# Turning a job's rows between the steps of the job before: a mixture of experts on one Trainium2 core

## The chip, the core and the metric

The kernel runs on one core of a Trainium2 chip. A core has a matmul engine (TensorE, PE in the profile, with its weight loads as PEld), VectorE (DVE), ScalarE (ACT), GpSimd (POOL) and a queue engine (SyncE, SP), each with its own stream of instructions, done in order and tied to the others by semaphores. The metric is the time of one execution in microseconds of device time, as the median of some runs.

## The reference

First a spectral layer on x of 8 x 1856 x 256: a Fourier transform over the sequence, a complex 256x256 product with a bias, a soft threshold, and the transform back. Its 14848 rows then go through a mixture of 16 experts in 4 groups, one expert for each row:

```
g_idx = argmax(x @ w_group);        g_w = softmax weight of that group
e_idx = argmax(xg @ w_expert[g]);   e_w = softmax weight of that expert
h  = maximum(xg[mask_e] @ w1[g, e], 0.0)      # 256 -> 1024
ye = h @ w2[g, e]                             # 1024 -> 256
out[tok_idx] = (g_w * e_w)[:, None] * ye
```

All is float32. The kernel makes each fp32 product from high and low parts (names ending in h and l): high x high, high x low and low x high.

## The kernel before

Until about 470 us the spectral layer, the routing and the first rows of four experts run in an order written out as a string of letters. From there on one loop goes over 40 **jobs**; the order on every engine is that of the program text. A job is one expert (or a part of one) with a fixed number of rows. Jobs 0 to 39 have these rows, bars standing between experts: 256, 304 | 432 | 400 | 384, 384, 336 | 256, 256 | 384, 384, 320 | 384, 384, 288 | 256, 384, 336 | 256, 384, 288 | 256, 384, 288 | 256, 384, 256 | 256, 384, 256 | 256, 320, 256 | 256, 320, 256 | 416, 384 | 320, 384.

What job i does, in the order of the text:

- The **second layer** of job i-1 (`down`, L695 and L696) for its first two tiles of 128 rows; for some row counts it is done turned instead (`turned_g`, L717), whole, with `back_g` (L730, L736, L738) bringing the result back during the job after.
- The **first layer** of job i (`up_g`): 8 steps f = 0 to 7 of six matmuls each (L619). After each step ACT makes hh, the high half of the hidden rows (L624), and DVE hl, the low half (L627). The second layer needs all hh and hl.
- Between the steps: the **gathers** of job i+2 (`deal_g`; POOL reads rows from memory into xg, L560; SP then deals them to the tile xm in blocks of 32 rows by 8 to 16 DMAs, L572), and the **weight pieces**. `split_w` lists eight pieces for the next expert's weights, each a cast on ACT (L524) and a subtraction on DVE (L525). In jobs 3, 5, 7, 10, 13, 16, 19, 22, 25, 28, 31, 34 and 36 such a list starts. With 384 rows or more and no older pieces one is emitted behind every step, all eight within the job; with fewer rows one behind every second step, and the other four in the job after.
- Behind the loop: pieces left over, then `dma_next` (SP loads the next expert's weights into the buffers that the pieces were read from, L512, and its row list, L1107 and L1109), then `turn_rows` for job i+1: DVE transposes xm in blocks of 32x32 into xtf, in four instructions (L582), ACT casts xtf to xth (L588), DVE subtracts to xtl (L589). Both are the first layer's input in job i+1. From job 4 on all jobs get their rows so, which makes 36 groups of four transposes.
- Then the rest of the second layer of job i-1, its third tile, if there is one.

The first layer writes to five PSUM buffers in turn, xm and xg have two and three buffers, xtf has one, the raw weights two.

Of the kernel before, what the change touches and what calls it, by code (L numbers as in the profile page):

```python
# [136 lines left out]
def spectral_moe(ctx: ExitStack, tc: tile.TileContext, x, wri, bri, wgate, w1, w1q, w2, cst, out):  # L137
# [179 lines left out]
    moved, heads, turns, parked = [], [], [], []  # L317
# [124 lines left out]
    def drain(gen):  # L442
        for _ in gen:
            pass
# [90 lines left out]
    def fetch(mp, ids, bufs, rows=NPAD + 1, late=False):  # L535
        n = ids.n
        out_ = []
        for c0 in range(0, n, 2):
            w = min(2, n - c0)
            xg = mp.tile([128, 2, D], F32, name="xg", bufs=bufs)  # L540
            for c in range(w):
                m = ids.rows(c0 + c)
                ins = nc.gpsimd.indirect_dma_start(
                    out=xg[0:m, c, :], out_offset=None, in_=ys_d[0:rows, :],
                    in_offset=bass.IndirectOffsetOnAxis(ap=ids.gi[0:m, c0 + c:c0 + c + 1], axis=0))
                if late:
                    behind(ins, "stores of the early jobs go first")
            out_.append((xg, w, ids.rows(c0 + w - 1)))
        return out_
# [23 lines left out]
            yield  # L573
        res.append(xm.rearrange("p c b d -> p (c b) d"))

    def turn_rows(xm, ids):
        n = ids.rows()
        xt = xq.tile([128, 2, 8, 64], F32, name="xtf", bufs=1)
        for a_ in range(2):
            k = (n - 32 * a_ + 63) // 64  # L580
            for to in range(2):
                nc.vector.transpose(out=xt[64 * to:64 * to + 64, :, 0:k, 32 * a_:32 * a_ + 32].rearrange("f b c t -> f c b t"),  # L582
                                    in_=xm[64 * a_:64 * a_ + 64, 0:k, 64 * to:64 * to + 64].rearrange("t c (b f) -> t c b f", b=2))
        xth = xq.tile([128, 2, n], F32R, name="xth")
        xtl = xq.tile([128, 2, n], F32R, name="xtl")
        xt = xt.rearrange("p b c t -> p b (c t)")
        for ts in [slice(i, min(n, i + 256)) for i in range(0, n, 256)]:
            nc.scalar.copy(out=xth[:, :, ts], in_=xt[:, :, ts])  # L588
            nc.vector.tensor_tensor(out=xtl[:, :, ts], in0=xt[:, :, ts], in1=xth[:, :, ts].bitcast(F32), op=ALU.subtract)  # L589
        return xth, xtl  # L590

    def prep(mp, xgs, n, bufs=None):
        xth = mp.tile([128, 2, n], F32R, name="xth", bufs=bufs)
# [16 lines left out]
    def up_g(pp, xt2, n, wt, hs):  # L610
        xth, xtl = xt2
        w1h, w1l = wt[0], wt[1]
        for f in range(8):
            o = pp.tile([128, 512], F32, name="ph")
            fs = slice(f * 128, (f + 1) * 128)
            k = 0
            for ch in range(2):
                for a_, b_ in ((w1h, xth), (w1h, xtl), (w1l, xth)):
                    nc.tensor.matmul(o[:, :n], lhsT=a_[:, ch, fs], rhs=b_[:, ch, 0:n], start=k == 0, stop=k == 5)  # L619
                    k += 1  # L620
            hh, hl = hs
            cuts = [slice(i, min(n, i + 256)) for i in range(0, n, 256)]
            for cs in cuts:
                ins = nc.scalar.activation(out=hh[:, f, cs], in_=o[:, cs], func=AF.Relu)  # L624
            step_end[:] = [ins.ins.name]
            for cs in cuts:
                nc.vector.scalar_tensor_tensor(out=hl[:, f, cs], in0=o[:, cs], scalar=0.0, in1=hh[:, f, cs].bitcast(F32),  # L627
                                               op0=ALU.max, op1=ALU.subtract)
            yield
# [29 lines left out]
    def h_tiles():  # L659
        return hq.tile([128, 8, WIDE], F32R, name="hh"), hq.tile([128, 8, WIDE], F32R, name="hl")  # L660
# [44 lines left out]
    def down(*args):  # L705
        drain(down_g(*args))
# [37 lines left out]
    jobs = [(0, 0), (0, 1), (1, 0), (1, 1), (0, 2), (1, 2), (2, NF), (3, NF)]  # L744
# [671 lines left out]
    def of(k):  # L1416
        return [("r", (k, i)) for i in range(len(CUTS[k]))]

    def fixed(e):
        return [("l", (e, i)) for i in range(len(FCUTS[e]))]  # L1420

    jobs = fixed(3) + fixed(1) + fixed(2) + of(0) + fixed(0)
# [4 lines left out]
    raws, jids, jw, rids, ready = {}, {}, {}, {}, {}  # L1427
# [23 lines left out]
    prev, behind_, todo, ahead = None, iter(()), [], {}  # L1451
    DEALT = jobs.index(("r", (0, 0)))
    x2 = prep(xq, first[0], jids[0].rows())
# [5 lines left out]
    for i, (kind, q) in enumerate(jobs):  # L1459
        ids = jids[i]  # L1460
        if kind == "r":
            wt = wts["r", q[0]] = jw[i] if i in jw else wts["r", q[0]]
        else:
            wt = wts[q[0]] = jw[i] if i in jw else wts[q[0]]
        nxt = fetch(xp2, jids[i + 1], 3, late=i == 0) if i + 1 < DEALT else None
        rest, back = iter(()), behind_
        behind_ = iter(())
        if prev is not None:
            pids = prev[1]
            if turned(i - 1):  # L1470
                yt = xq.tile([128, 2, WIDE], F32, name="yt", bufs=1)
                rest = turned_g(psy, "py", prev[0], pids, prev[2], yt)
                drain(rest)
                behind_ = back_g(psy, "py", yt, pids, "out")
            else:
                n2 = min(2, pids.n)
                down(psy, "py", prev[0], pids, prev[2], "out", range(n2))
                rest = down_g(psy, "py", prev[0], pids, prev[2], "out", range(n2, pids.n))
        ready.pop(i, lambda: None)()
        gathers = iter(())  # L1480
        if DEALT <= i + 2 < len(jobs):
            if jobs[i + 2][0] == "r":
                k, part = jobs[i + 2][1]
                jids[i + 2] = rids[k][part]
            ahead[i + 2] = []
            gathers = deal_g(jids[i + 2], ahead[i + 2])
        every = 1 if todo or ids.rows() < 384 else 0
        if i in split_at:
            jw[split_at[i]], todo = split_w(raws.pop(split_at[i]))
        hs = h_tiles()  # L1490
        for f, _ in enumerate(up_g(psh, x2, ids.rows(), wt, hs)):
            if f % 2:
                next(back, None)
            else:
                next(gathers, None)
            if f % 2 or not every:
                emit(todo, 1)
            for _ in range(1 if i else 3):
                next(table, None)
        if i not in split_at or not every:  # L1500
            emit(todo, len(todo))
        if i == 0 or i in split_at:
            dma_next(i)
        if nxt is None and i + 1 < len(jobs):
            x2 = turn_rows(ahead.pop(i + 1).pop(), jids[i + 1])
        drain(gathers)
        drain(rest)
        prev = (hs, ids, wt)
        if nxt is not None:
            x2 = prep(xq, nxt, jids[i + 1].rows())  # L1510
# [11 lines left out]
    with tc.For_i(KF, nfx, 1) as iv:  # L1522
        rw, ids = flex_load(bass.ds(iv, 1))
# [7 lines left out]
        wt, ids = half_load(bass.ds(iv, 1))  # L1531
# [45 lines left out]
```

## Time and profile before

| | us |
|---|---|
| median of three runs | 1068.2 |
| the three runs | 1068.2, 1059.08, 1074.6 |
| the profiled execution | 1074.4 |
| its span, first to last instruction | 1072.6 |
| busy in the span: PE | 1024.9 (96%) |
| DVE | 742.3 (69%) |
| ACT | 484.4 (45%) |
| POOL | 434.0 (40%) |

The span is what the trace covers; the remaining 1.8 us of the profiled execution lie around it. Matmuls are pipelined and their ends are modelled, so the start times of two matmuls tell more than the busy time. In a timeline a row is: start, duration, engine, line, operation, output and input tiles with partitions and elements, number of instructions merged, and in brackets the idle time of the engine ahead of it with what ended it.

### The profile page before, as it was taken

What the parts mean: (1) busy time and instruction counts of PE and PEld (TensorE: products, weight loads), DVE (VectorE), ACT (ScalarE), POOL (GpSimd) and SP (SyncE); (2) the same over time, 40 slices, a digit from 0 to 9 for tenths busy, and PEclk for the clock granted to TensorE, in tenths of its full rate; (3) what the DMA queues carried; (4) which work ended last, traced back from release to release, by engine and by line L of the source; (5) the groups of instructions that cost most, each with busy time, mean ns of one, the idle gap of its engine ahead of it and who ended that gap; (6) DMA issues with size and microseconds to landing.
All of it is one profiled execution on the core that took longest, in us unless ns stands there. A gap on an engine that the chain in (4) does not pass through costs nothing.

```text
span 1072.6 us, 25269 instructions
## 1 busy us (share of the span) xinstructions
PE 1024.9 (96%) x9496; PEld 888.0 (83%) x9496; DVE 742.3 (69%) x1754; ACT 484.4 (45%) x1273; POOL 434.0 (40%) x600
## 2 busy tenths in 40 slices
PE   8999999999999999999999999999999999999996
PEld 4886767776867888889988899979998898999995
DVE  6879999999998665436566665665665656767652
ACT  2664645545636243234344444444544535445532
POOL 0120164465463657633235324334342343443432
PEclk9999999999999999989999999999998999999998
DMA  9402512412314320312342442433424244244210
GB/s 383 146 2 91 187 42 106 152 63 81 121 60 180 122 105 28 126 53 67 126 139 79 142 140 72 137 88 126 146 68 135 62 146 140 70 143 139 79 52 29
DMA packets 63407, 117.25 MB, mean 109 GB/s; under 512 B 20588, under 2 KB 44473, under 8 KB 56754
## 3 DMA queue, kind: packets, MB, share of 16 engines
q1 hardware_dynamic: 46450, 67.81, 19.7%
q0 software_dynamic: 11936, 30.79, 9.0%
q10 hardware_dynamic: 4896, 17.01, 4.1%
q8 instruction: 76, 1.25, 0.5%
q14 instruction: 49, 0.40, 0.1%
HBM read 71.37 MB, written 32.46 MB: 97 GB/s over the span
## 4 chain that ended last, share of the span: by engine, by line
PE 61%; DVE 17%; issue 8%; POOL 4%; DMA 3%; SPq 3%; ACT 2%; another core or an unknown queue 0%; ACTq 0%; POOLq 0%; DVEq 0%
PE ph L619 20%; PE py L695 8%; PE pw L887 5%; PE py L717 5%; PE py L696 4%; SPq L572 3%; PE ph L1047 2%; PE pw L869 2%; PE bank L805 2%; PE bank L911 2%; PE bank L929 2%; DVE big L525 2%; DVE hl L627 2%; PE bank L435 2%; DVE big L439 2%
## 5 line engine op out<-in xcount | busy, mean ns | idle before, releaser
L619 PE MATMUL ph<-xth,big 128*128 128x256 f32 (+8 forms) x1280 | 291.7, 312 | 3.8 <-ACT xth L588 3.0
L627 DVE SCALAR_TENSOR_TENSOR hl<-ph,hh 128x256 fp32r<-128x256 f32 (+8 forms) x528 | 167.6, 355 | 132.6 <-ACT hh L624 78.4
L624 ACT ACTIVATE hh<-ph 128x256 fp32r<-128x256 f32 (+8 forms) x528 | 151.2, 339 | 182.1 <-PE ph L619 134.0
L695 PE MATMUL py<-big,hh 128*128 128x512 f32 (+2 forms) x608 | 222.5, 404 | 1.9 <-ACT hh L624 1.4
L619 PEld LDWEIGHTS ph<-xth,big 128*128 128x128 f32 x1280 | 216.6, 188 | 7.6 <-ACT xth L588 5.0
L619 PE MATMUL ph<-xtl,big 128*128 128x256 f32 (+8 forms) x640 | 199.1, 311 | 2.8 <-DVE xtl L589 2.4
L669 POOL DMA_INDIRECT out_dram<-yo,si_r x92 | 92.6, 1006 | 251.0 <-DVE yo L701 204.7
L696 PE MATMUL py<-big,hl 128*128 128x256 f32 (+2 forms) x608 | 175.5, 289 | 5.2 <-DVE hl L627 4.8
L695 PEld LDWEIGHTS py<-big,hh 128*128 128x128 f32 (+2 forms) x608 | 115.7, 190 | 30.3 <-ACT hh L624 2.3
L560 POOL DMA_INDIRECT xg<-ys_d,gi_r x92 | 93.7, 1018 | 89.7 <-ACT hh L624 60.5
L696 PEld LDWEIGHTS py<-big,hl 128*128 128x128 f32 (+2 forms) x608 | 116.0, 191 | 10.4 <-DVE hl L627 10.1
L619 PEld LDWEIGHTS ph<-xtl,big 128*128 128x128 f32 x640 | 120.4, 188 | 5.1 <-DVE xtl L589 4.3
L717 PE MATMUL py<-hh,big 128*128 128x320 f32 (+4 forms) x320 | 75.2, 319 | 1.4 <-DVE yo L701 1.2
L588 ACT CAST xth<-xtf 128x512 fp32r<-128x512 f32 (+5 forms) x59 | 28.4, 518 | 106.6 <-DVE xtf L582 106.6
L582 DVE STREAM_TRANSPOSE xtf<-xm 64x384 f32<-64x384 f32 (+3 forms) x144 | 72.9, 506 | 3.4 <-DMA xm<-xg 2.0
L525 DVE TENSOR_TENSOR big<-xt,big 128x512 fp32r<-128x512 f32 x104 | 71.0, 682 | 5.7 <-ACT big L524 4.4
L853 POOL TENSOR_TENSOR xdl<-xd,xdh 128x512 fp32r<-128x512 f32 (+1 forms) x23 | 28.0, 1217 | 107.4 <-ACT xdh L846 87.1
L887 PE MATMUL pw<-wh,xh 128*128 128x256 f32 x240 | 66.6, 300 | 2.8 <-DVE pw L877 2.8
L524 ACT CAST big<-xt 128x512 fp32r<-128x512 f32 x104 | 65.4, 629 | 0.0
L892 ACT ACTIVATE big<-pw,nlam 128x512 f32<-128x512 f32 x60 | 41.3, 689 | 46.4 <-PE pw L887 45.5
L887 PE MATMUL pw<-wl,xh 128*128 128x256 f32 x240 | 62.0, 280 | 0.0
L887 PEld LDWEIGHTS pw<-wh,xh 128*128 128x128 f32 x240 | 45.1, 188 | 16.9 <-DVE pw L877 7.5
(263 smaller groups left out, 2004.1 us busy)
## 6 DMA issues: line engine op xcount, KB each, us to landing
xt<-in_w_dram SPq DMA_DIRECT2D x21, 1024.0 KB
ys_d<-ysb ACTq DMA_DIRECT2D x32, 512.0 KB
xt<-in_w1q_dram SPq DMA_DIRECT2D x13, 1024.0 KB
xm<-xg SPq DMA_DIRECT2D x290, 32.0 KB
big<-in_x_dram SPq DMA_DIRECT2D x8, 1024.0 KB
xt<-in_x_dram SPq DMA_DIRECT2D x8, 1024.0 KB
xm<-xg SPq DMA_DIRECT2D x144, 16.0 KB
xg<-ys_d,gi_r POOLq DMA_INDIRECT x92
```

Of the source, the lines that this page charges most:

```text
L524: nc.scalar.copy(out=wt[:, 2 * i, cs], in_=raws[i][:, cs])
L525: nc.vector.tensor_tensor(out=wt[:, 2 * i + 1, cs], in0=raws[i][:, cs], in1=wt[:, 2 * i, cs].bitcast(F32), op=ALU.subtract)
L560: ins = nc.gpsimd.indirect_dma_start(out=xg[0:m, c, :], out_offset=None, in_=ys_d[0:NPAD + 1, :], in_offset=bass.IndirectOffsetOnAxis(ap=i ...
L582: nc.vector.transpose(out=xt[64 * to:64 * to + 64, :, 0:k, 32 * a_:32 * a_ + 32].rearrange("f b c t -> f c b t"), in_=xm[64 * a_:64 * a_ + ...
L619: nc.tensor.matmul(o[:, :n], lhsT=a_[:, ch, fs], rhs=b_[:, ch, 0:n], start=k == 0, stop=k == 5)
L624: ins = nc.scalar.activation(out=hh[:, f, cs], in_=o[:, cs], func=AF.Relu)
L627: nc.vector.scalar_tensor_tensor(out=hl[:, f, cs], in0=o[:, cs], scalar=0.0, in1=hh[:, f, cs].bitcast(F32), op0=ALU.max, op1=ALU.subtract)
L669: ins = nc.gpsimd.indirect_dma_start(out=out, out_offset=bass.IndirectOffsetOnAxis(ap=ids.si[0:ids.rows(t), t:t + 1], axis=0), in_=ysb, in ...
L695: nc.tensor.matmul(o, lhsT=hh[:, f, ts], rhs=w2b[:, :, f, :], start=f == 0, stop=f == 7, skip_group_check=True)
L696: nc.tensor.matmul(o[:, 0:D], lhsT=hl[:, f, ts], rhs=w2h[:, f, :], start=False, stop=f == 7, skip_group_check=True)
L717: nc.tensor.matmul(o, lhsT=w_[:, f, ds_], rhs=h_[:, f, 0:n], start=f == 0 and h_ is hh and w_ is w2h, stop=f == 7 and h_ is hh and w_ is n ...
L887: ins = nc.tensor.matmul(y, lhsT=a_[:, h, k % 2, j], rhs=t[:, j, h], start=False, stop=a_ is xl and h == 1, skip_group_check=True)
```

## The change

`turn_rows` becomes a generator, `turn_g`, that yields after each of its four transposes and appends its result to a list. In each job it is made ahead of the first layer's loop and advanced by one behind steps 4, 5, 6 and 7, ahead of what `back`, the gathers and the pieces emit in that step. What is left of it, the cast to xth and the subtraction to xtl, follows right behind the loop, ahead of pieces left over and of `dma_next`.

```
-    def turn_rows(xm, ids):
+    def turn_g(xm, ids, res):
...
                 nc.vector.transpose(out=xt[...], in_=xm[...])
+                yield
...
-        return xth, xtl
+        res.append((xth, xtl))
...
         hs = h_tiles()
+        turns, turning = [], iter(())
+        if i + 1 in ahead:
+            turning = turn_g(ahead.pop(i + 1).pop(), jids[i + 1], turns)
         for f, _ in enumerate(up_g(psh, x2, ids.rows(), wt, hs)):
+            if f >= 4:
+                next(turning, None)
             if f % 2:
                 next(back, None)
...
+        drain(turning)
         if i not in split_at or not every:
             emit(todo, len(todo))
         if i == 0 or i in split_at:
             dma_next(i)
-        if nxt is None and i + 1 < len(jobs):
-            x2 = turn_rows(ahead.pop(i + 1).pop(), jids[i + 1])
+        if turns:
+            x2 = turns.pop()
         drain(gathers)
         drain(rest)
```

## Rows read from the trace of the kernel before

**Rows 1.** The page's costliest groups: busy, mean ns of one, idle before, releaser.

```profile
L619 PE MATMUL ph<-xth,big 128*128 128x256 f32 (+8 forms) x1280 | 291.7, 312 | 3.8 <-ACT xth L588 3.0
...
L619 PE MATMUL ph<-xtl,big 128*128 128x256 f32 (+8 forms) x640 | 199.1, 311 | 2.8 <-DVE xtl L589 2.4
...
L696 PE MATMUL py<-big,hl 128*128 128x256 f32 (+2 forms) x608 | 175.5, 289 | 5.2 <-DVE hl L627 4.8
...
L582 DVE STREAM_TRANSPOSE xtf<-xm 64x384 f32<-64x384 f32 (+3 forms) x144 | 72.9, 506 | 3.4 <-DMA xm<-xg 2.0
```

**Rows 2.** Timeline of PE: second layer of job 9, first layer of job 10.

```profile
604.17 0.39 PE L695 MATMUL py<-big,hh 128*128 128x512 f32 x1
...
609.70 0.28 PE L696 MATMUL py<-big,hl 128*128 128x256 f32 x1
610.93 0.44 PE L619 MATMUL ph<-xth,big 128*128 128x384 f32 x1 [0.96 <-ACT xth L588]
611.69 0.45 PE L619 MATMUL ph<-xtl,big 128*128 128x384 f32 x1 [0.31 <-DVE xtl L589]
611.97 0.51 PE L619 MATMUL ph<-xth,big 128*128 128x384 f32 x2
```

**Rows 3.** Timeline of DVE, jobs 8 and 9, up to job 10's transposes.

```profile
590.23 0.42 DVE L627 SCALAR_TENSOR_TENSOR hl<-ph,hh 128x256 fp32r<-128x256 f32 x1 [0.48 <-ACT hh L624]
...
591.01 0.69 DVE L525 TENSOR_TENSOR big<-xt,big 128x512 fp32r<-128x512 f32 x1
...
601.77 0.62 DVE L627 SCALAR_TENSOR_TENSOR hl<-ph,hh 128x256 fp32r<-128x256 f32 x2 [0.44 <-issue]
...
607.54 2.33 DVE L582 STREAM_TRANSPOSE xtf<-xm 64x384 f32<-64x384 f32 x4 [1.96 <-DMA xm<-xg]
```

**Rows 4.** Timeline of DVE, last steps of job 16.

```profile
718.58 0.61 DVE L627 SCALAR_TENSOR_TENSOR hl<-ph,hh 128x256 fp32r<-128x256 f32 x2
...
719.71 0.61 DVE L627 SCALAR_TENSOR_TENSOR hl<-ph,hh 128x256 fp32r<-128x256 f32 x2
```

**Rows 5.** Timeline of PE, second layer of job 16.

```profile
720.18 0.39 PE L696 MATMUL py<-big,hl 128*128 128x256 f32 x1 [0.52 <-DVE hl L627]
```

**Rows 6.** Timelines of DVE and PE: last hl of job 19, its user.

```profile
764.50 0.61 DVE L627 SCALAR_TENSOR_TENSOR hl<-ph,hh 128x256 fp32r<-128x256 f32 x2
...
765.70 0.28 PE L696 MATMUL py<-big,hl 128*128 128x256 f32 x1
```

**Rows 7.** Chain that ended last: start, duration, what; job 10's last row DMAs.

```profile
605.27 0.59 SPq L572
...
606.54 1.76 DMA xm<-xg
```

**Rows 8.** Timeline of SP's queue around job 8.

```profile
591.73 0.33 SPq L512 DMA_DIRECT2D xt<-in_w_dram  x1
...
594.39 35.39 SPq L572 DMA_DIRECT2D xm<-xg  x44
```

**Rows 9.** Timeline of SP's queue, jobs 32 to 36.

```profile
949.86 0.33 SPq L512 DMA_DIRECT2D xt<-in_w_dram  x1
...
988.26 0.33 SPq L512 DMA_DIRECT2D xt<-in_w_dram  x1
...
1001.81 1.22 SPq L572 DMA_DIRECT2D xm<-xg  x2
```

**Rows 10.** Timeline of DVE, steps 4 and 7 of job 36.

```profile
999.64 0.65 DVE L627 SCALAR_TENSOR_TENSOR hl<-ph,hh 128x256 fp32r<-128x256 f32 x2
...
1006.42 0.66 DVE L627 SCALAR_TENSOR_TENSOR hl<-ph,hh 128x256 fp32r<-128x256 f32 x2 [3.20 <-remote]
```

**Rows 11.** Stages of job 16's end: us, busy by engine, granted clock, DMA share.

```profile
716.00:720.70 4.70, 2.90 (x10) 1.60 (x11) 4.70 (x13) 3.43 (x11) 0.46 (x2) 1.00 0.25 53
720.70:724.70 4.00, 4.00 (x16) 3.44 (x15) 3.22 (x8) 1.22 (x3) 0.00 (x0) 0.57 0.64 209
```

**Rows 12.** Timeline of ACT, job 16, step 3.

```profile
713.28 0.55 ACT L624 ACTIVATE hh<-ph 128x256 fp32r<-128x256 f32 x2 [1.85 <-PE ph L619]
```

## The prediction

> **What bounds the kernel now.** I read the page first: TensorE (PE) against the others, then the rows of its first matmuls in each job, since the change hands them their input. The first layer and the second layer form one stream of matmuls on PE, and in the job stage hardly anything else ends last. What PE still waits for is in [rows 1]: 3.0 us for the high half of a job's input (L588), 2.4 us for the low half (L589), and 4.8 us for the low halves of the hidden rows (L627). Then I read PE by start times, because a booked idle time is shorter than what is lost. At the start of job 10 [rows 2] the matmul after 609.70 was due at 609.82, the third one, at 611.97, was due 2 x 0.173 later, at 610.17: 1.80 us are lost where the rows book 0.96 + 0.31. The same kind of wait, with 0.5 to 1.8 us, stands in front of eight jobs (6, 9, 10, 14, 16, 20, 29 and 36). Then I read VectorE (DVE) in the job before such a start, and the queue of SyncE (SP) that brings the rows it turns.
>
> **A. What moving the transposes can give back.** The path to a job's input is now: last hl of the job before, four transposes, cast on ScalarE (ACT), subtraction on DVE. Afterwards only the fourth transpose stands behind the last hl, so the path is shorter by three; one takes 506 ns on the mean [rows 1], for a job of 384 rows 2.33/4 = 0.58 us [rows 3]. Three, 1.5 us, are about what the eight waits are long. They go, except where DVE itself is late. Price: the 5.4 us of [rows 1], times 1.80/1.27 for what the rows don't book: 7.7 us. Ends: 0 (all of them are late by B) and 7.7. I take 7.7.
>
> The second half of the change, the split ahead of pieces left over, I cost at nothing. Where eight pieces are due in a job, all eight are emitted within the loop; where four are, the other four go into the next job's loop; the list is empty whenever the call behind the loop is reached. The cast on ACT and the subtraction on DVE so keep their place among other instructions, but for the last piece, which now comes behind the fourth transpose. No instruction is added or removed, and the transposes issue no DMA.
>
> **B. What stands behind the three transposes on DVE.** DVE works in the order of the program. Transposes 1 to 3 now run ahead of the hl of steps 5, 6 and 7, and the next second layer needs these. In a job with eight weight pieces DVE makes one hl and one piece per 1.13 us (718.58 to 719.71, [rows 4]), while PE feeds a step of 384 rows in 6 x 0.173 = 1.04 us, and a step of the second layer in 0.35. So DVE is behind at the end of each such job. In job 16 PE waits for exactly these hl, 0.52 us of 1.13 [rows 5]. Each transpose put there moves the end of the last hl, and so PE, by its own length. Jobs 5, 16, 22, 25 and 28 show such a wait at their end: 5 x 3 x 0.506 = 7.6 us. In job 19 the last hl starts at 764.50 and takes 0.61, PE needs it at 765.70 [rows 6]: 0.59 us to spare against 1.52, costs 0.93. Read in the same way job 13 has 0.1 to spare and pays 1.4, job 10 has 1.4 and pays 0.1. In sum 10.0. In the smaller jobs 8, 15, 21, 34 and 35 the same count (pieces every second step) gives 0.15 to 1.35 each, about 3.4 together, less certain. Ends: 5 (only the five, and a third absorbed by waits that are there anyway) and 13.4. I take 12. Nothing in other jobs: DVE rests 0.44 us per step in a job without pieces [rows 3], and most such jobs have a third tile of the job before behind their loop.
>
> **C. Rows that are not there yet.** This is the added wait: a transpose now waits for its rows in the middle of the loop, and behind it on DVE are queued the hl of steps 5 to 7 (PE waits for them), the pieces (the weight buffer and so SP's next weight load wait for them) and the yo additions. In the trace one group waits: job 10's, at 607.54, idle 1.96 for xm [rows 3]. The hl of step 4 starts at 601.77 there, and so the first transpose would stand from 602.4 to 607.5, as the DMAs that it reads are issued up to 605.27 and the last one lands 1.76 after 606.54 [rows 7]. Then transposes and hl alternate, 0.58 and 0.55: the last hl ends at 607.54 + 3 x 0.58 + 3 x 0.55 = 610.9. PE, which begins the second layer of job 9 at 604.17 [rows 2], needs it 7 x 0.35 + 0.23 later, at 606.9: 4.0 us. And the rows come later still. SP's second weight load of job 7 starts at 591.73 [rows 8], right behind the last piece, which starts at 591.01 and takes 0.69 [rows 3]; the DMAs of job 10's rows are behind it on the same queue, from 594.39. With four transposes in front of that piece, 4 x 0.58, less the 0.48 us that DVE rests ahead of 590.23 [rows 3], it ends 1.8 us later: 4.0 to 5.8. The same pattern is at 949.86 (rows for job 34) and at 988.26 (rows for job 37, last issued behind 1001.81) [rows 9]. In job 36 the first transpose would be due at 1000.3 and get its rows at about 1003.0; its last hl, now at 1006.42 after a 3.20 us gap of ACT [rows 10], comes 1.4 later by the same count (transpose 0.58, piece 0.60, hl 0.57 in turn), with the shift 3.2. Job 33: 0.4 to 2.0. Together 5.8 to 11.0; I take 9, as the piece's delay is sure and its passing on to the rows likely.
>
> [...]
>
> **Sum.** -7.7 + 12 + 9 = +13.3 us. The profiled execution took 1074.4 us, its span being 1072.6 with 1.8 around it; its successor would take 1087.7. The three runs have their median at 1068.2, 0.6% lower, and 13.3 us are carried over as they are: 1081.5 us, +1.2%. Runs of the same kernel differ by 15 us here, so about 2% is what a measurement can tell from no change.
>
> **Rivals.** First, the other side: the waits of A go and B and C don't come. Its place is DVE's rest: if the transposes fit into DVE's gaps in steps 4 to 7, and the rows are there, PE loses nothing: 1068.2 - 7.7 = 1060.5. It decides at one point, whether the last hl of a job ends before PE's eighth pair of the second layer. For it: the gaps of 0.44 us per step in the jobs without pieces, and the one of 3.20 us in job 36. Against it: DVE is busy 4.70 of 4.70 us in the tail of job 16 [rows 11], with PE waiting. Chance 0.17.
>
> Second, slower by more: the new waits are worth more than their length because TensorE's clock falls. [...] Against it: jobs 16, 22 and 25 pay this already, so that it can come anew only at the others. [...] Chance 0.17.
>
> Third, the change does not do what it says: waits of ACT and SP that are tied to time and not to DVE absorb B and C as well as A: 1068. For it: ACT itself is late in the middle of job 16, by 1.85 us at 713.28 [rows 12], though PE had gone on by then. Chance 0.12.
>
> Forecast: chance 0.54.
>
> **How the numbers follow.** 1081. The range goes from the first rival's time to the second's, 1060 to 1095, which also takes in the ends of A to C (5 + 5.8 - 7.7 = +3 and 13.4 + 11 - 7.7 = +17). Slower by over 2% is above 1089.6: most of the second rival and the forecast's upper end, 0.2. Faster by over 2%, below 1046.8, would need more than all of A: 0.02. The rest, 0.78.
>
> **What would show it.** Right: the transposes stand between the hl of steps 4 to 7; PE's idle ahead of L619 for L588 and L589 falls from 5.4 us to below 2; its idle ahead of L696 and L717 for L627 rises by more than 5; a transpose in job 9 waits for xm for over 4 us, one in job 36 for over 2; job 10's rows are issued later than 594 to 606, measured from the start of job 8. Wrong: the rows of job 10 are there at step 4 of job 9; or DVE's last hl in jobs 16, 22, 25 and 28 ends no later against PE than before.

## The result, and the profile after

The changed kernel takes 1079.6 us (median of four runs, 1077.4 to 1083.8) against 1068.5 us for the kernel before (median of four, three of them those on record ahead): a ratio of 1.0117 [1.0084, 1.015] (the quotient of the medians is 1.0104), 11 us slower, where 1081 (+13.3 us) was forecast. The two profiled executions stand only 3.0 us apart (spans 1072.6 and 1075.6), because the one of before lies above its median and the one of after below. So parts are compared place by place, and the size of the whole is taken from the medians. Lines of the code behind the new function have moved by one: L588, L589, L619, L627 and L696 of before are L589, L590, L620, L628 and L697 of after.

The page of the kernel after, costliest groups, which answer to [rows 1]:

```profile
L620 PE MATMUL ph<-xth,big 128*128 128x256 f32 (+8 forms) x1280 | 290.9, 311 | 0.7 <-ACT xth L607 0.7
...
L620 PE MATMUL ph<-xtl,big 128*128 128x256 f32 (+8 forms) x640 | 198.3, 310 | 0.4 <-DVE xtl L608 0.4
...
L697 PE MATMUL py<-big,hl 128*128 128x256 f32 (+2 forms) x608 | 177.8, 292 | 15.3 <-DVE hl L628 12.9
...
L582 DVE STREAM_TRANSPOSE xtf<-xm 64x384 f32<-64x384 f32 (+3 forms) x144 | 72.8, 506 | 19.8 <-DMA xm<-xg 16.4
```

Read the last column. What PE still waits for ahead of the first layer belongs to an earlier stage (L607, L608); the 3.0 + 2.4 us for a dealt job's input are gone. In exchange PE waits 12.9 us instead of 4.8 for the low halves of the hidden rows, and DVE itself stands 16.4 us instead of 2.0 in front of transposes whose rows haven't come. Those 16.4 us are five places: jobs 9 (4.20), 24 (2.08), 27 (2.17), 33 (4.36) and 36 (3.54).

Timeline of DVE after, jobs 8 and 9, the stretch of [rows 3]:

```profile
588.41 0.69 DVE L525 TENSOR_TENSOR big<-xt,big 128x512 fp32r<-128x512 f32 x1
...
598.45 0.62 DVE L628 SCALAR_TENSOR_TENSOR hl<-ph,hh 128x256 fp32r<-128x256 f32 x2 [0.43 <-ACT hh L625]
603.27 0.57 DVE L582 STREAM_TRANSPOSE xtf<-xm 64x384 f32<-64x384 f32 x1 [4.20 <-DMA xm<-xg]
603.77 0.58 DVE L628 SCALAR_TENSOR_TENSOR hl<-ph,hh 128x256 fp32r<-128x256 f32 x2
604.36 0.57 DVE L582 STREAM_TRANSPOSE xtf<-xm 64x384 f32<-64x384 f32 x1
604.97 0.62 DVE L628 SCALAR_TENSOR_TENSOR hl<-ph,hh 128x256 fp32r<-128x256 f32 x2
605.62 0.57 DVE L582 STREAM_TRANSPOSE xtf<-xm 64x384 f32<-64x384 f32 x1
606.22 0.62 DVE L628 SCALAR_TENSOR_TENSOR hl<-ph,hh 128x256 fp32r<-128x256 f32 x2
```

Timeline of PE after, second layer of job 9:

```profile
602.57 0.40 PE L696 MATMUL py<-big,hh 128*128 128x512 f32 x1
604.21 0.40 PE L697 MATMUL py<-big,hl 128*128 128x256 f32 x1 [1.24 <-DVE hl L628]
604.44 0.40 PE L696 MATMUL py<-big,hh 128*128 128x512 f32 x1
605.45 0.39 PE L697 MATMUL py<-big,hl 128*128 128x256 f32 x1 [0.61 <-DVE hl L628]
605.67 0.53 PE L696 MATMUL py<-big,hh 128*128 128x512 f32 x1
606.70 0.58 PE L697 MATMUL py<-big,hl 128*128 128x256 f32 x1 [0.51 <-DVE hl L628]
607.08 0.63 PE L696 MATMUL py<-big,hh 128*128 128x512 f32 x1
```

One transpose waits, and three hl stand behind it on DVE; PE stops in front of each of them. The L696 at 607.08 would have been due at 603.62 (602.57 and three pairs of 0.35): 3.46 us lost, of which the rows book 2.36. Then each pair takes 0.64 instead of 0.35 for a while. The view by stretches of the kernel after shows why (us, busy time of PE, PEld, DVE, ACT, POOL, granted clock, DMA share, GB/s):

```profile
600.00:607.50 7.50, 5.14 (x23) 3.73 (x22) 4.04 (x10) 1.06 (x4) 0.93 (x1) 0.89 0.27 63
607.50:613.00 5.50, 5.50 (x20) 4.81 (x19) 1.47 (x4) 1.78 (x4) 1.04 (x1) 0.54 0.21 54
613.00:620.00 7.00, 7.00 (x42) 7.00 (x41) 6.16 (x17) 6.30 (x19) 4.54 (x5) 1.00 0.18 56
```

Behind the stretch in which PE was busy for 5.14 of 7.50 us the granted clock is 0.54 of full speed for 5.5 us, and 1.00 in the stretch after that: by estimate 0.46 x 5.5 = 2.5 us more. A wait of 3.5 us has cost 6.

The queue of SP after, around job 8, which starts at 577.13 here and at 581.89 before:

```profile
589.13 0.33 SPq L512 DMA_DIRECT2D xt<-in_w_dram  x1
...
591.79 38.55 SPq L572 DMA_DIRECT2D xm<-xg  x44
```

Counted from the start of job 8 the rows begin at 14.7 us, before at 594.39 - 581.89 = 12.5 [rows 8]: 2.2 us later. The piece that releases the weight load (DVE at 588.41, ending 589.10) now has four transposes ahead of it, and the load starts right behind its end. But job 9 itself starts as much later (15.3 us after job 8, before 13.1), because job 8's second layer takes 9.64 us instead of 7.48: it waits for hl behind transposes too. Against job 9's own start the rows begin 0.6 us ahead in both kernels. So in this execution the 4.20 us come from the early place alone; where the changed kernel was run again (experiment 11) the rows begin 0.96 us behind job 9's start, and the wait is 5.80.

**How long each second layer takes** is the measure that separates the parts of the prediction best: the time from its first matmul to the first matmul of the next first layer, worked out from PE's timelines (one profiled execution per kernel). Undisturbed it takes 5.60 to 5.65 us with two tiles and 8.47 with three. "Lost" is the sum above that. The experiments are told below; "after again" is experiment 11, the last four lines are from a second chip.

```
job                5    13     16    19     22     25    28  lost |     9    24     27     33  lost
undisturbed     8.47  8.47   5.65  5.65   5.65   5.65  5.65       |  5.65  5.60   5.62   5.62
before         10.22  8.74  10.56  5.64  11.58   9.71  6.63  17.9 |  6.76  5.60   5.62   5.62   1.1
e1 (order)      9.82  9.37   9.94  5.66  10.26   8.15  6.66  14.7 |  6.96  5.61   5.63   5.63   1.3
after           8.45  8.47  10.98  6.62   7.52   7.39  6.51  10.8 | 11.40  7.20   7.30   9.98  13.4
after again     10.23 8.47   7.96  6.60   6.64   7.38  6.46   8.6 | 12.69  6.90  10.06  12.15  19.3
e2 (late rows) 10.41  8.47   7.72  6.60   7.54  12.03  7.85  15.4 |  7.15  5.60   5.63   7.04   2.9
e3 (pieces)     9.78  8.47   7.11  5.70   7.05   7.91  5.65   6.5 |  9.06  6.89   5.62  10.11   9.2
e4 (loads)     12.02  8.48  10.03  6.59   8.46   7.19  6.49  14.1 |  5.64  5.61   9.83   5.62   4.2
e10 (load)      8.47  8.47  10.75  6.59   7.45   6.58  6.49   9.6 |  5.65  7.18   7.56   5.62   3.5
e12 (no move)   8.48  8.48   7.68  5.64   6.91   6.91  5.65   4.6 |  6.16  5.60   5.62   5.62   0.5
e5 (C alone)    8.47  8.48   5.64  5.64   5.65   5.65  5.65   0.0 | 12.84  7.17   7.68   6.27  11.5
e6 (8,32,35)    8.48  8.48   5.64  5.64   5.65   5.64  5.65   0.0 |  8.13  6.18   6.29   6.64   4.8
e7 (neither)    8.47  8.48   5.64  5.64   5.65   5.64  5.65   0.0 |  7.80  5.61   6.50   5.62   3.0
e8 (no move)    8.48  8.48   5.65  5.64   5.65   5.64  5.65   0.0 |  7.61  6.25   7.40   5.62   4.4
```

The left jobs are those of part B of the prediction, the right ones those in which a transpose waits for rows (C). The right half follows the edits, with two exceptions: in experiment 3 job 27 is undisturbed though its transposes stay early, and in experiment 2 job 33 loses 1.4 with its transposes behind the loop. The left half has another source of lost time too, as large as the change's or larger, at jobs 5, 16, 22 and 25: the kernels with the early place there (after twice, e2, e4, e10) lose 8.6 to 15.4 us, and those with the late place (before, e1, e3) 6.5 to 17.9, though before and e1 give every engine the same instructions in the same order. On the second chip this source is missing. Job 8, which is in neither half, belongs to B as well: 7.48 and 7.58 before and in e1, 9.64 and 7.63 after and after again, 5.61 in e7.

### The profile page after: what moved, and what is told of

The parts are those of the page before. It is cut to its first block, busy times and chain, and to the rows that moved or that the text cites. A ratio compares the mean times of both kernels' runs of the same rounds, so it can differ in the third digit from the quotient of the medians.

```text
span 1075.6 us, 25256 instructions
## 1 busy us (share of the span) xinstructions
PE 1024.3 (95%) x9496; PEld 889.3 (83%) x9496; DVE 746.7 (69%) x1754; ACT 488.5 (45%) x1273; POOL 437.5 (41%) x600
## 3 DMA queue, kind: packets, MB, share of 16 engines
q1 hardware_dynamic: 46450, 67.81, 19.8%
## 4 chain that ended last, share of the span: by engine, by line
PE 65%; DVE 14%; DMA 5%; issue 5%; SPq 4%; POOL 3%; ACT 3%; ACTq 0%; DVEq 0%; POOLq 0%
PE ph L620 20%; PE py L696 10%; PE py L718 6%; PE py L697 5%; PE pw L888 5%; SPq L572 4%; PE ph L1048 2%; PE bank L806 2%; PE pw L870 2%; PE bank L912 2%; PE bank L930 2%; PE bank L435 2%; DVE big L439 1%; PE bank L962 1%; PE bank L1071 1%
## 5 line engine op out<-in xcount | busy, mean ns | idle before, releaser
L620 PE MATMUL ph<-xth,big 128*128 128x256 f32 (+8 forms) x1280 | 290.9, 311 | 0.7 <-ACT xth L607 0.7
L628 DVE SCALAR_TENSOR_TENSOR hl<-ph,hh 128x256 fp32r<-128x256 f32 (+8 forms) x528 | 170.0, 355 | 83.9 <-ACT hh L625 57.6
L696 PE MATMUL py<-big,hh 128*128 128x512 f32 (+2 forms) x608 | 224.2, 406 | 0.5 <-DVE yo L702 0.5
L620 PEld LDWEIGHTS ph<-xth,big 128*128 128x128 f32 x1280 | 217.1, 188 | 3.0 <-ACT xth L607 0.9
L620 PE MATMUL ph<-xtl,big 128*128 128x256 f32 (+8 forms) x640 | 198.3, 310 | 0.4 <-DVE xtl L608 0.4
L697 PE MATMUL py<-big,hl 128*128 128x256 f32 (+2 forms) x608 | 177.8, 292 | 15.3 <-DVE hl L628 12.9
L696 PEld LDWEIGHTS py<-big,hh 128*128 128x128 f32 (+2 forms) x608 | 116.7, 192 | 27.7 <-DVE yo L702 0.7
L697 PEld LDWEIGHTS py<-big,hl 128*128 128x128 f32 (+2 forms) x608 | 116.9, 192 | 24.0 <-DVE hl L628 20.6
L620 PEld LDWEIGHTS ph<-xtl,big 128*128 128x128 f32 x640 | 120.7, 189 | 0.7 <-DVE xtl L608 0.6
L582 DVE STREAM_TRANSPOSE xtf<-xm 64x384 f32<-64x384 f32 (+3 forms) x144 | 72.8, 506 | 19.8 <-DMA xm<-xg 16.4
L589 ACT CAST xth<-xtf 128x512 fp32r<-128x512 f32 (+5 forms) x59 | 28.4, 518 | 96.8 <-DVE xtf L582 88.6
L702 DVE SCALAR_TENSOR_TENSOR yo<-py,ent_r,yo 128x256 f32<-128x256 f32 (+1 forms) x66 | 31.6, 481 | 57.0 <-ACT yo L701 50.3
```

The source lines that it names most:

```text
L696: nc.tensor.matmul(o, lhsT=hh[:, f, ts], rhs=w2b[:, :, f, :], start=f == 0, stop=f == 7, skip_group_check=True)
L697: nc.tensor.matmul(o[:, 0:D], lhsT=hl[:, f, ts], rhs=w2h[:, f, :], start=False, stop=f == 7, skip_group_check=True)
```

## The experiments

Three groups, each on one chip with the kernel before beside it. On the first chip the kernel before took 1072.5 us, on the second 1044.4, on the third 1068.4. Ratios are against it. Diffs are against the changed kernel unless said otherwise; i is the job, f the step of its first layer. In the expectations the rows theory says that the loss is part C of the prediction, rows that aren't there yet, and the queue theory that it is part B, hl pushed back in DVE's queue.

**1. The second half of the change alone** (first chip). The transposes go back behind the loop; only the order of the last pieces is the new one.

```diff
-            if f >= 4:
-                next(turning, None)
```

> The transposes stay behind the loop in one block; only the second half of the change is kept, the cast and subtraction ahead of pieces left over. Both theories (rows late, and hl pushed back) say: the list of pieces is empty there, so every engine gets the instructions of the kernel before in the same order, 1068 us, ratio 1.000 within 0.004. It also tells how far two equal streams of instructions lie apart. A third theory, that this order matters: more than 5 us away.

Measured: 1072.1 us, 1.0012 [0.9987, 1.0037]. DVE's wait for rows is 2.2 us in one place, as before. The order of the instructions on every engine is that of before; only the names of a few tiles differ. The split ahead of the pieces left over costs nothing because nothing is left over.

**2. Late rows turned behind the loop** (first chip): jobs 9, 24, 27, 33 and 36 keep the old place.

```diff
-            if f >= 4:
+            if f >= 4 and i not in (9, 24, 27, 33, 36):
```

> The changed kernel, but in jobs 9, 24, 27, 33 and 36, where its trace shows a transpose waiting for xm (16.4 us on VectorE in all), the four transposes stand behind the loop again. Rows theory: the loss is mostly there, PE gets back 3.9 + 1.6 + 1.7 + 4.4 + 1.6 = 13 us and pays some 2 us at the starts of jobs 10 and 34 again: 1068 to 1070 us, ratio to before about 1.00. Queue theory (three transposes of 1.5 us ahead of the last hl are the loss, in all jobs with pieces): only job 36 of these has pieces, 1077 to 1079 us, ratio 1.009.

Measured: 1075.9 us, 1.0043 [1.0018, 1.0069]. The loss in jobs 9, 24, 27 and 33 falls to 2.9 us, and the time comes down to about half of the change's loss, short of the ratio of 1.00 that the rows theory gave and well under the 1.009 of the queue theory. In its execution other places lose: job 34's second layer takes 4.0 us more than after, job 10's first layer 2.1 and job 25's second 4.6.

**3. The jobs with many pieces behind the loop** (first chip), the places of B.

```diff
-            if f >= 4:
+            if f >= 4 and i not in (5, 7, 10, 13, 16, 19, 22, 25, 28, 31, 34):
```

> The changed kernel, but in jobs 5, 7, 10, 13, 16, 19, 22, 25, 28, 31 and 34, which have weight pieces in every or every second step and whose rows come in time, the transposes stand behind the loop again. Queue theory: the pushed hl of these jobs cost 8 to 12 us, and the waits at the starts of jobs 6, 14, 20 and 29 come back with 4: 1072 to 1076 us. Rows theory: nothing to gain here, the waits come back, 1080 to 1084 us.

Measured: 1076.7 us, 1.0053 [1.0026, 1.0079]. The ratio lies in the queue theory's range (1072 to 1076 us against the 1068.5 of the result is 1.003 to 1.007) and below that of the rows theory (1.011 to 1.015). Job 19 is back at 5.70 from 6.62 and job 28 at 5.65 from 6.51 (before it took 6.63). Over the seven jobs 6.5 us are lost, less than in any kernel that keeps the early place there (8.6 to 15.4), but the kernel before, with the late place as well, lost 17.9, so these sums don't size B. The ratio of the change, 1.0117 in the result and 1.0079 on the third chip, is 0.6 or 0.3% higher: by this estimate B costs 3 to 7 us beyond the start waits that come back. The intervals of experiments 2 and 3 overlap, so the medians alone don't say which part is the larger.

**4. All of the weight load behind the rows** (first chip).

```diff
-        if i == 0 or i in split_at:
+        if i == 0 or i in split_at and i not in (7, 31, 34):
             dma_next(i)
...
         drain(gathers)
+        if i - 1 in (7, 31, 34):
+            dma_next(i - 1)
```

> The changed kernel with its transposes in the loops, but the weight loads that SP issues at the end of jobs 7, 31 and 34, and that stand there until the last carried piece is done, are issued one job later, behind the DMAs of the rows. Rows theory: rows for jobs 10, 34 and 37 are there in time, the waits of 4.2, 4.4 and 3.5 us on VectorE are gone, about 10 us less: 1068 to 1071 us, and the rows that follow are not later. Queue theory: 1079 us as the changed kernel. Should the weights come too late by this, a wait ahead of L524 shows in jobs 12, 36 or 38.

Measured: 1093.8 us, 1.0214 [1.0185, 1.0243]. The waits in jobs 9 and 33 go (both second layers are back at their old length), but what the moved call loads, the weights and the row list, now comes too late. Timelines of experiment 4, POOL and PE in job 34, ACT and PE in job 36:

```profile
970.93 0.19 POOL L354 CAST gi_r<-ent_r 128x7 int32<-128x7 f32 x1 [10.35 <-DMA ent_r<-lst]
...
978.67 0.60 PE L620 MATMUL ph<-xth,big 128*128 128x320 f32 x1 [4.24 <-DVE yo L702]
...
1017.88 0.62 ACT L524 CAST big<-xt 128x512 fp32r<-128x512 f32 x1 [8.26 <-DMA xt<-in_w1q_dram]
...
1019.94 0.68 PE L620 MATMUL ph<-xth,big 128*128 128x416 f32 x1 [4.67 <-DVE hl L628]
```

PE stops 4.2 and 4.7 us in the middle of two first layers. In job 36 ACT stands in front of a piece whose weights haven't landed. In job 34 POOL waits for the row list, the stores behind it on POOL are late, and ACT waits 9.29 us for one of these. As a test of what the rows' delay costs it failed: it trades one late transfer for another.

**5. Only the late rows early** (second chip), the counterpart of experiment 2: the five jobs of C are the only ones with transposes in the loop.

```diff
-            if f >= 4:
+            if f >= 4 and i in (9, 24, 27, 33, 36):
```

> The kernel before, with transposes between the steps in jobs 9, 24, 27, 33 and 36 alone, where the rows came late. Rows theory: VectorE stands ahead of the first transpose in jobs 9, 33 and 36 for 3 to 5 us each, less than in the changed kernel since the last carried piece of the job before isn't delayed; PE loses 2.2 + 1 to 2 + 1.4 there, 0 to 3 in jobs 24 and 27: 5 to 8 us, ratio to before 1.005 to 1.0075. Queue theory: only job 36 has pieces, 1.5 us, ratio 1.0015.

Measured: 1056.7 us, 1.0125 [1.0098, 1.0152]; DVE waits 15.5 us for rows in six places, in job 9 alone 5.95. C alone costs 12 us here, more than the rows theory's 5 to 8, and as much as the whole change on the chip of the result. The whole change wasn't run on this chip, and no run has only the transposes of the jobs with pieces early: B alone is untested.

**6. Only the jobs with a carried list of pieces** (second chip), those in front of three of the late ones.

```diff
-            if f >= 4:
+            if f >= 4 and i in (8, 32, 35):
```

> The kernel before, with transposes between the steps in jobs 8, 32 and 35 alone, the jobs whose last carried piece lets SP's second weight load go. If the delay is passed on to the rows: that load and the rows for jobs 10, 34 and 37 come 1.8 us later, the start of job 10 waits 2 us longer and that of job 34 about 1, the starts of jobs 9 and 36 lose their waits of 1.5 each, and the hl of job 8 are pushed: 0 to +4 us, ratio 1.000 to 1.004. If it is not passed on: 1.5 to 2.5 us faster, ratio 0.998.

Measured: 1049.5 us, 1.0051 [1.0032, 1.007]. Of the transposes that it moves only one waits for its rows, 1.06 us in job 8, and it costs 5 us all the same, a little more than was expected: what is delayed in jobs 8, 32 and 35 is passed on to the next job through SP's queue. Job 32 shows it against experiment 7, which leaves these jobs alone; it starts at 918.97 in experiment 6 and at 924.17 in experiment 7. SP's queue in experiment 6, then in experiment 7:

```profile
928.28 0.33 SPq L512 DMA_DIRECT2D xt<-in_w_dram  x1
...
931.46 13.55 SPq L572 DMA_DIRECT2D xm<-xg  x14
```

```profile
931.67 0.33 SPq L512 DMA_DIRECT2D xt<-in_w_dram  x1
...
933.80 8.15 SPq L572 DMA_DIRECT2D xm<-xg  x12
```

The load starts 9.31 us after the job instead of 7.50 and the rows 12.49 instead of 9.63: a delay of 1.8 us has become one of 2.9 us for the rows, and job 33's transposes, which stand behind the loop in both, wait 2.56 us for them instead of not at all.

**7. Neither** (second chip): only jobs with no part in B, in C or in experiment 6.

```diff
-            if f >= 4:
+            if f >= 4 and i in (3, 4, 6, 11, 12, 14, 15, 17, 18, 20, 21, 23, 26, 29, 30, 37, 38):
```

> The changed kernel without both suspects: transposes between the steps only in 17 jobs that have no pieces and whose rows come in time (3, 4, 6, 11, 12, 14, 15, 17, 18, 20, 21, 23, 26, 29, 30, 37 and 38; job 3 has pieces, but a long second layer behind it). If rows and queue are all there is: within 3 us of the kernel before, ratio 0.997 to 1.001, the wait at the start of job 16 gone. If something third costs time: above 1.004.

Measured: 1046.2 us, 1.0014 [1.0003, 1.0026]. That is just above the range of "rows and queue are all there is" and far from that of a third cause. Part of it is C again: on this chip the rows of jobs 18 and 21 are late too, their transposes wait 1.71 and 1.86 us, and job 21's second layer takes 6.89 us instead of 5.64. Where DVE has rest and the rows are there, the move costs next to nothing and brings nothing.

**8. The pieces moved instead** (second chip, later once more on the third). From the kernel before: where a list of pieces is carried over from the job ahead, it goes into steps 0 to 3 of the next loop, and what is still left comes behind the transposes. These stay behind the loop.

```diff
+        carried = bool(todo)
...
-            if f % 2 or not every:
+            if f < 4 if carried or not every else f % 2:
                 emit(todo, 1)
...
+        if nxt is None and i + 1 < len(jobs):
+            x3 = turn_rows(ahead.pop(i + 1).pop(), jids[i + 1])
         if i not in split_at or not every:
             emit(todo, len(todo))
...
-            x2 = turn_rows(ahead.pop(i + 1).pop(), jids[i + 1])
+            x2 = x3
```

> The kernel before with its transposes behind the loop, but pieces moved instead: in jobs with eight pieces four go behind steps 0 to 3 and four behind the cast and subtraction; in the jobs with four carried pieces they go behind steps 0 to 3. Queue theory: the last hl no longer stand behind pieces, the waits of L696 for L627 (4.8 us on the page, more with what follows at the lower clock) and of the job starts (5.4) go: 8 to 16 us faster, ratio 0.985 to 0.993. Rows theory: the carried pieces end 2 us earlier and with them the rows for jobs 10, 34 and 37, 1.8 us at the start of job 10: ratio 0.998. If pieces behind the turn push the yo additions: slower, and PE waits for psum ahead of L695.

Measured on the second chip: 1044.2 us, 1.0006 [0.9991, 1.0021], no gain, which neither theory had. Rows make transposes behind the loop wait there as well, for 9.2 us in all.

**9. The transposes four steps earlier** (third chip): the dose of C.

```diff
-            if f >= 4:
+            if f < 4:
```

> The changed kernel with its transposes behind steps 0 to 3 instead of 4 to 7. Rows theory: four steps earlier (3 to 4 us) the rows of many more jobs are not there, VectorE's waits for xm grow from 16 to some 50 us and PE loses about 30: ratio 1.02 to 1.04. Queue theory: the pushed hl have four more steps to catch up, so less is lost: 1.000 to 1.006.

Measured: 1105.6 us, 1.0329 [1.0292, 1.0366]. The page of experiment 9, from an execution of 1114.1 us:

```profile
L582 DVE STREAM_TRANSPOSE xtf<-xm 64x384 f32<-64x384 f32 (+3 forms) x144 | 73.0, 507 | 60.9 <-DMA xm<-xg 50.6
```

Some 50 us of waiting were expected and 50.6 came, in 14 places instead of 5; in job 9 alone DVE stands still for 8.93 us ahead of one transpose, against 4.20 after. Against the changed kernel on the same chip (experiment 11) DVE waits 31 us longer (50.6 against 19.8), and the median is 26 us longer (1105.6 against 1079.7): most of the wait reaches the end. It now falls into the first layers: that of job 9 takes 16.64 us, after 8.38.

**10. Half of the weight load behind the rows** (third chip): behind jobs 7 and 31 the second matrix is loaded one job later, so that the gathered rows come ahead of it on SP's queue. DVE's order stays that of the changed kernel.

```diff
-    def raw_w(e, first=w1):
+    def raw_w(e, first=w1, part=slice(0, 2)):
...
-            raws[j] = raw_w(ek, w1q)
+            raws[j] = raw_w(ek, w1q, slice(0, 1 if later else 2))
+            if later:
+                return lambda: raws[j].extend(raw_w(ek, w1q, slice(1, 2)))
...
+        if second:
+            second()
+            second = None
...
-            dma_next(i)
+            second = dma_next(i, i in (7, 31))
```

> The changed kernel, but of the weight loads issued at the end of jobs 7 and 31 only the second half, which has to wait for the last carried piece, is issued one job later, behind the DMAs of the rows; the first half stays (both halves, in job 34 too, made the weights come late). Rows theory: the rows for jobs 10 and 34 no longer stand behind that piece, the waits of 4.2 and 4.4 us on VectorE fall below 1.5 each, 6 to 8 us less than the changed kernel, ratio to before 1.003 to 1.007. Queue theory: as the changed kernel.

Measured: 1071.6 us, 1.0042 [1.0009, 1.0074]. The queue of SP in experiment 10:

```profile
590.12 10.27 SPq L572 DMA_DIRECT2D xm<-xg  x16
600.73 0.28 SPq L512 DMA_DIRECT2D xt<-in_w_dram  x1
```

And its timeline of DVE, where the transpose of job 9 stands:

```profile
601.61 0.62 DVE L628 SCALAR_TENSOR_TENSOR hl<-ph,hh 128x256 fp32r<-128x256 f32 x2 [0.43 <-issue]
602.14 0.56 DVE L582 STREAM_TRANSPOSE xtf<-xm 64x384 f32<-64x384 f32 x1
602.65 0.62 DVE L628 SCALAR_TENSOR_TENSOR hl<-ph,hh 128x256 fp32r<-128x256 f32 x2
```

The second load no longer stands in front of the rows. The transposes of job 9 wait no more, and the second layers of jobs 9 and 33 take 5.65 and 5.62 us, undisturbed. The place of the transposes alone does no harm there; it is the rows' time of arrival, and the queue sets that. The median is 8.1 us below the changed kernel beside it (1079.7). The two intervals against the kernel before overlap, but the two sets of runs differ directly, in their means by 5.8 us (1072.7 and 1078.5).

**11. The changed kernel once more** (third chip).

> The changed kernel once more, beside the others of this group, because two chips so far differ by 28 us in the kernel before and the earlier groups were run on different ones. Rows theory: 1.010 to 1.015 on any chip, since SP's queue sets when rows come, and the faster PE is elsewhere, the longer it waits for them. Queue theory: 1.012 where ScalarE is late in the middle of jobs 16, 22 and 25, under 1.005 where it isn't.

Measured: 1079.7 us, 1.0079 [1.0049, 1.0108]. Both medians are those of the result (1079.6, 1068.5), and their quotient, 1.0105, lies in both intervals, which overlap. The ratio lies below the rows theory's range, whose lower end is still in the interval. DVE waits 19.8 us for rows in six places.

**12. The kernel of experiment 8 again** (third chip, where the change was slower).

> The kernel before with eight pieces put behind steps 0 to 3 and behind the turn, once more: on a chip where ScalarE is late in the middle of jobs 16, 22 and 25 the last hl no longer stand behind pieces, 6 to 12 us faster, ratio 0.989 to 0.995; on one where it isn't, 1.000 as before.

Measured: 1056.3 us, 0.9883 [0.9851, 0.9915]: on this chip 12 us faster than the kernel before and 23 us faster than the changed one beside it. The page of experiment 12:

```profile
L696 PE MATMUL py<-big,hl 128*128 128x256 f32 (+2 forms) x608 | 172.6, 284 | 0.6
...
L582 DVE STREAM_TRANSPOSE xtf<-xm 64x384 f32<-64x384 f32 (+3 forms) x144 | 72.9, 506 | 3.3 <-DMA xm<-xg 1.5
```

Its timeline of DVE at the end of job 16, the stretch of [rows 4]:

```profile
711.42 2.21 DVE L627 SCALAR_TENSOR_TENSOR hl<-ph,hh 128x256 fp32r<-128x256 f32 x8 [1.75 <-ACT hh L624]
713.55 2.19 DVE L582 STREAM_TRANSPOSE xtf<-xm 64x384 f32<-64x384 f32 x4
716.48 0.93 DVE L589 TENSOR_TENSOR xtl<-xtf,xth 128x512 fp32r<-128x512 f32 x2 [0.74 <-ACT xth L588]
717.33 2.49 DVE L525 TENSOR_TENSOR big<-xt,big 128x512 fp32r<-128x512 f32 x4
```

The last hl run without a piece between them, then the transposes, then the pieces. PE's wait for hl falls from 5.2 us to 0.6. What has slack here is the pieces.

## Why the prediction was right, and which of its terms were not

The sign, the class and the size came out: +13.3 us forecast, 11.1 measured. A came out as costed, 7.4 us. That leaves by estimate 18.5 us (11.1 + 7.4) for B and C together, of 21 forecast. Place by place they didn't come out: a rule of B failed, C was too low at one place and missed two, and how the 18.5 split isn't settled. That the sum lies so near is in part luck.

**A, -7.7: right, 7.4.** The eight start waits are gone from the page (5.4 us to 0). In seven of the eight jobs the first layer can be read by itself: 6, 9, 10, 14, 16, 20 and 29 together took 55.88 us before and 51.40 after, 51.44 after again. With the waits ahead of the first matmul of jobs 10 and 14, which the table has as 6.76 - 5.65 and 8.74 - 8.47 in the second layers ahead of them, 4.5 + 1.4 = 5.9 us. Job 9's first matmul came at 595.01 before and was due at 594.19, 0.8 more, and job 36's first layer gave back 0.7: 7.4 us.

**The second half, 0: right** (experiment 1).

**B, +12: right on DVE and at job 19, wrong as a rule for PE, and not settled as a sum.** Job 19, costed at 0.93, pays 0.98 (5.64 to 6.62; 6.59 and 6.60 in the other kernels with the early place), and experiment 3 gives it back. But job 13 (1.4) pays nothing in any of these kernels, and the five jobs that were to pay 1.52 each on top of what PE waited before [rows 5] take 40.9 us together after, against 48.7 before and 44.8 in experiment 1. The step that failed: "Each transpose put there moves the end of the last hl, and so PE, by its own length." Its first half holds. Timeline of DVE after, job 16, the stretch of [rows 4]:

```profile
716.78 0.61 DVE L628 SCALAR_TENSOR_TENSOR hl<-ph,hh 128x256 fp32r<-128x256 f32 x2
717.43 0.51 DVE L582 STREAM_TRANSPOSE xtf<-xm 64x320 f32<-64x320 f32 x1
717.97 0.69 DVE L525 TENSOR_TENSOR big<-xt,big 128x512 fp32r<-128x512 f32 x1
718.58 0.61 DVE L628 SCALAR_TENSOR_TENSOR hl<-ph,hh 128x256 fp32r<-128x256 f32 x2
```

The hl are 1.80 us apart instead of 1.13, 0.67 more for a transpose of 0.51. The second half fails at job 13 and, in the execution after, at job 5 (8.45, undisturbed). In job 16 DVE was late before because the hh of ACT had come 1.85 us late in step 3 [rows 12]; in the execution after, ACT's longest gap ahead of an hh in this job is 0.62. Timeline of PE after, second layer of job 16:

```profile
715.69 0.40 PE L696 MATMUL py<-big,hh 128*128 128x512 f32 x1
717.26 0.39 PE L697 MATMUL py<-big,hl 128*128 128x256 f32 x1 [1.17 <-DVE hl L628]
...
719.05 0.58 PE L697 MATMUL py<-big,hl 128*128 128x256 f32 x1 [1.17 <-DVE hl L628]
```

The layer begins at 713.57, before at 714.18, and waits twice for 1.17 us, where before there were four waits for hl of 0.28 to 0.52, 1.80 in sum [rows 5], and one of 0.25 for hh. It takes 10.98 us against 10.56: 0.4 longer, not 1.5. So the two aren't the same kernel with and without three transposes: one has ACT's lateness and no early transposes, the other the reverse, and against the undisturbed 5.65 the layer loses 5.3 us after, the clock behind the two waits included (0.50 from 719.43 to 724.34). The other executions with the early place lose 2.1 to 5.1 there, and experiment 3, without it, 1.5. Two more readings of the prediction were off: jobs 15 and 21 have no pieces and lose 0.2 us each after, and job 8, one of the "0.15 to 1.35 each", takes 2.2 us longer after (0.15 after again), with its pairs at 0.64 us behind two waits (granted clock 0.50 from 588.82 to 592.03). What B costs in all stays open: 3 to 7 us by experiment 3 beyond the start waits that come back there, while the table's left half even falls from 17.9 to 10.8. The source that ACT's lateness has isn't told apart from it; it moves single jobs by up to 5 us between executions of related kernels.

**C, +9: the mechanism was right, its price too low at job 33, and two places missed.** The second layers of jobs 9, 24, 27 and 33 lose 13.4 us after and 19.3 after again, and job 36 1.6 more (its start to that of job 37: 20.41 to 21.98). Experiments 2, 5 and 10 give or take this with the place and with the arrival of the rows, experiment 9 raises it with the dose, and experiment 6 shows the passing on. As a sum C is 13.4 + 1.6 = 15 us in the one execution and 19.3 + 3.2 = 22.5 in the other, 12 by experiment 5 beyond the start waits that go there, and 4 to 8 by the ratio of experiment 2 beyond those that come back.
- Job 9 was costed at 4.0 to 5.8 us of waiting. PE lost 3.5 by waiting and 2.5 by the clock, 6.0, and its second layer is 5.75 above the undisturbed 5.65. The 1.8 us for rows that come later still didn't arise there in the execution after, as job 9 itself started later; the clock, which the term didn't have, took their place.
- Job 33 was costed at 0.4 to 2.0 and lost 4.4. Its first transpose would be due at 955.34, when the hl ahead of it ends (954.92 + 0.42), and gets its rows at 959.70. Measured from the start of job 33 (953.55 before, 950.19 after) SP begins with the rows 1.55 us ahead before (952.00) and 0.98 behind after (951.17), and issues the last of them 6.1 us behind before and 8.1 behind after: 2.0 to 2.5 us of the 4.36 are the shift of the rows, about 2 were in the place alone. The term had at most 2.0 for both.
- Jobs 24 and 27 were not in the sum. They lost 1.6 and 1.7. Their rows were there for transposes behind the loop, and so no row of before showed a wait; the arrival of rows had been followed at three jobs and not at every job.

VectorE did nothing in the 4.20 us ahead of 603.27, though the hh for the hl queued behind the transpose had been done at 600.51: what stood behind the waiting transpose waited with it, and that is what made this term.

**The rivals.** The first (no B, no C, 1060.5) fell: the transposes don't fit where the rows are late. The second, a falling clock at each new wait, was right as a mechanism and wrong in extent. Before, the clock was down at jobs 16, 22 and 25 (0.57 [rows 11], 0.50 from 810 to 816 us, 0.50 from 858 to 860). After, it is 2.5 us of 6 at job 9, and jobs 8 and 16 show it too (clock 0.50, pairs at 0.64 us), but its mean over the span only goes from 0.986 to 0.983, by estimate 3 us. The range's upper end, 1095, lies 14 us above the forecast for this rival; no run shows these 14. The third fell as a whole (1068); whether waits that were there took in part of B, as at jobs 5 and 13, the runs don't tell. Parts don't add up to the whole: C alone costs 1.0125 on the second chip, and taking C or B out of the change on the first leaves 1.0043 and 1.0053. A wait that is taken away at one place lets another show, as job 34 does in experiment 2.

**What would show it.** Start waits below 2: 0. Waits for hl up by more than 5: 4.8 to 12.9. Job 9's transpose over 4 us: 4.20. Job 36's over 2: 3.54. Rows later against the start of job 8: 2.2 us, though not against that of job 9. Of the two signs against it the second came in part: over jobs 16, 22, 25 and 28 PE's second layers took 32.4 us against 38.5 before.

## What to carry to other kernels

An instruction that is moved ahead on an engine that works in order, as VectorE did here, brings the arrival time of its input with it, and everything behind it waits for that (at job 9 4.20 us, with three hl behind); so look up when the input lands in each place where it will stand, not only where a wait shows today, and which queue brings it. Here the queue was part of the loop: the moved instruction delayed a piece, the piece held a weight load, and the load stood in front of the very rows that the next job's transposes need. When two kinds of work compete ahead of a deadline, move the kind that has slack; here that was the pieces, which gave 1.2% on one chip and nothing on another.

## What was not expected of the hardware

The same kernel before took 1044.4 us on one chip and 1068.4 and 1072.5 on two others, 2.3 and 2.7% more, which is more than any edit but that of experiment 9 made. Part of the difference stands where ACT's hh come late: in the kernel of experiment 8, which ran on both kinds, the second layers of jobs 16, 22 and 25 take 5.65, 5.65 and 5.64 us on the second chip, undisturbed, and 7.68, 6.91 and 6.91 on the third. Its timeline of ACT on the third chip names a releaser, PE, and 1.89 us:

```profile
710.84 1.89 ACT L624 ACTIVATE hh<-ph 128x256 fp32r<-128x256 f32 x8 [1.89 <-PE py L696]
```

What makes ACT late there wasn't tried and stays open. It decides what such a change is worth: on the chip where ACT wasn't late, the gain of experiment 12 was not to be had.
